# x loaded once for transposing and for the convolution, its copies to U moved to the start, and the gate's products moved back

## The chip, the cores and the metric

The kernel runs on one core of a Trainium2 chip. The core has TensorE (PE, matrix products into the PSUM accumulators), VectorE (DVE), ScalarE (ACT), GpSimd (POOL), and SyncE (SP), which here only issues transfers (DMA) between DRAM and the on-chip memory SBUF. Each engine works through its own list of instructions in order and waits on semaphores for the others. A matrix product has two operands: one is loaded as weights (PEld), the other streams through.

The metric is the device time of one execution in microseconds (us). The kernel before took 517.04 us, the median of three runs (515.87 to 517.63).

## The reference

One input x (2048 positions, 448 features) goes two ways, and a gate mixes the results:

```python
g = sigmoid((x * gate_w).sum(-1, keepdims=True))
a = attention(x)      # q = x@wq: 16 heads of 28; one k and one v head shared by all
                      # softmax(q k^T / sqrt(28)) v, then @ wo
b = ssm_conv(x)       # K[d,l] = Re sum_n C[d,n] exp(dt A[d,n])^l dt B[d,n], n < 256
                      # causal convolution of x[:,d] with K[d,:] by FFT, plus x * Dskip
return g * a + (1 - g) * b
```

Every output needs all 2048 by 2048 scores of 16 heads, that is 67 million exponentials, and for each of the 448 features a kernel K of 2048 values and a causal convolution with it.

## The kernel before, in words

**A planner.** The kernel writes its work down as operations with an engine, a cost in ns, what they read and write, and a priority (`Prog.op`, `Prog.dma`). `Prog.schedule` then plays the work through with those costs and fixes the order of instructions on each engine; what runs on the chip is that order, with semaphore waits between engines. A smaller `pr` goes first among operations that can start at the same time. `pg.after[i] = j` keeps operation i from being ordered before j without a wait on the chip. Constants such as `HEAD`, `NEED` and `AHEAD` shape the planner's choices; `PORT` charged VectorE for long GpSimd operations. So a change of a cost, a priority or a constant can reorder instructions everywhere.

**Attention.** The 2048 positions of queries are cut into 4 blocks of 512 (`qc`), the 16 heads into 4 groups of 4. For each of these 16 pairs there are 64 tiles: 16 key blocks of 128 times 4 heads. A tile's scores, 128 keys by 512 queries, fill one PSUM bank. Tiles are worked on in sets of 3 and 2 in turn (`sets`): TensorE writes their scores to banks 0 to 4, one ScalarE exponential (L1263) turns the whole set into weights `expT`, and TensorE multiplies these with the values into `psB` (L1278). The scores come in two forms: row-packed (`row`, L1231), in which heads use 32 rows each of the array and run side by side, and full-height (`full`, L1240), which reads `qM`, a copy of the queries with zeros in the other heads' rows. `qM` is filled by transfers on GpSimd's queue (L142). Sets 0 to 5 and, from set 24 on, the sets of three are row-packed. After 64 tiles `norm` divides by the sums, and `outp` and `fold` multiply with wo and the gate and add to `O`, the output in SBUF.

**The state-space part.** From the parameters VectorE builds, by repeated multiplication, tables of powers (`masters`, `tables`: L901 to L985) for 32 features at a time; TensorE makes the kernels K from them (`kgen`, L1005), which are written to DRAM (`KP_scratch`) and read back as shifted rows (`tload`, L1041); TensorE convolves with them (`conv`, L1065). The data operand is `U`, x in an order in which position residues lie side by side, with 16 zeros after each 16 values for the odd half. The results are multiplied by 1 - g (`omq`, L1080), turned (L1091) and added to `O`.

**The start.** `loads` brings x in four blocks of 512 positions, in which each partition gets 4 neighbouring rows (3584 bytes). `prep_x` transposes them on TensorE (L652), copies the results to `xT` on ScalarE and VectorE (L661, L663), makes the keys (L666, L676) with their largest absolute values (L673), and, through `Wv`, the values and the gate's sum into `psB` (L693). From the keys' maxima a bound is made (L697, L703, L704: `Wb`), which the first queries need: `qproj` makes a block's queries (L864), their absolute values (L870), the bound's product (L873) and the copy `qT` (L876). After that come the first scores and the first exponential. The copies that spread wq, wv and the gate's weights into `Wq` and `Wv` (L580 to L586) are on VectorE.

Meanwhile `prep_params` makes the seeds. The phase dt * A_im / 2 pi (L804) is brought into range by adding and subtracting a large constant (`MAGIC`) and a subtraction, both on GpSimd (L807, L808); ScalarE takes two sines (L810, L813); the cosine is 1 - 2 sin^2 of the half angle, again on GpSimd (L829, L830). The tensor dt * A_re ("t0") is another L804, `T<-psX,cst`, of which ScalarE makes six exponentials (L821, L824).

`prep_gate` makes 1 - g in the convolution's order: the value copy `vaug` (L712), the exponential (L717), three small VectorE steps (L719 to L721), then products with the identity (L736) and with selection matrices (L746) on TensorE, and the copy `omq`.

`fill` makes `U`: it loads x a second time, in the convolution's order, into `O` (16 transfers of 128 pieces of 896 bytes), and eight GpSimd copies (L611) interleave that into `U`; a transfer then copies U's even partitions to the odd ones, shifted by 16, and another clears `O`. U's zeros are four GpSimd memsets (L493, `consts`).

## Time and profile before

| | |
|---|---|
| median of three runs | 517.04 us |
| the profiled execution | 516.12 us |
| its span, first to last instruction | 514.4 us |
| ScalarE busy | 486.2 us |
| of it exponentials of scores (410 instructions) | 467.4 us |
| VectorE busy | 456.5 us |
| TensorE busy | 449.5 us |
| GpSimd busy | 176.8 us |
| first exponential of scores starts | 24.34 us |
| last exponential of scores ends | 508.2 us |
| mean granted TensorE clock | 0.959 |

How the lines are read: a timeline line gives the start and the length in us, the engine, the line of the kernel, the operation, output and input tiles with their shapes, how many instructions are merged in it, and in square brackets the engine's idle time before it and who ended that. A waits line gives the waiting instruction, what it waited for, the time in all, how often, and the longest. A line with two times and a colon is a stretch of the span with each engine's busy time in it, the granted clock, the busy share of the transfer engines, and GB/s. The granted clock is TensorE's, 1.00 being full speed.

### The profile page before, as it was taken

How to read it: one execution, taken by the hardware profiler on the slowest of the kernel's cores; microseconds unless marked ns; L12 is line 12 of the kernel's file. 1: busy time of each engine (PE TensorE's matmuls, PEld its weight loads, DVE VectorE, ACT ScalarE, POOL GpSimd, SP SyncE). 2: the span in 40 equal slices, each digit the busy share in tenths (PEclk: the TensorE clock that was granted, in tenths of full speed). 3: DMA queues.
4: the chain of work that ended last, by engine and by line, in shares of the span. 5: the costliest groups of instructions: out<-in, count | busy, mean ns of one | idle time of the engine just before them, and what ended most of it. 6: DMA issues, size and time to landing. Idle time of an engine off the chain costs nothing.

```text
span 514.4 us, 18888 instructions
## 1 busy us (share of the span) xinstructions
PE 449.5 (87%) x8456; PEld 197.2 (38%) x8456; DVE 456.5 (89%) x819; ACT 486.2 (95%) x436; POOL 176.8 (34%) x311
## 2 busy tenths in 40 slices
PE   7739779798888989989988999998899899999886
PEld 5403113143333434334443444443343444344453
DVE  4997999989999999999999999999999999821534
ACT  5677999999999999999999999999999999999995
POOL 8991122532232541424242233334252233334000
PEclk9957986979999999999999999999999999999999
DMA  9956920679989599899999999699999969999982
GB/s 238 234 146 43 135 61 22 190 215 342 354 255 303 183 335 319 269 349 290 369 337 349 348 310 368 199 313 370 369 335 331 369 204 369 286 371 330 370 284 46
DMA packets 117315, 140.29 MB, mean 273 GB/s; under 512 B 49945, under 2 KB 56506, under 8 KB 117234
## 3 DMA queue, kind: packets, MB, share of 16 engines
q1 hardware_dynamic: 108384, 129.72, 78.6%
q0 software_dynamic: 8704, 9.25, 6.8%
q8 instruction: 66, 1.08, 0.9%
q14 instruction: 15, 0.12, 0.1%
q10 hardware_dynamic: 146, 0.12, 0.1%
HBM read 127.24 MB, written 5.22 MB: 258 GB/s over the span
## 4 chain that ended last, share of the span: by engine, by line
ACT 40%; DVE 39%; PE 17%; issue 1%; DMA 1%; SPq 0%
ACT expT L1263 40%; DVE tab L958 6%; PE psS L1240 5%; PE psB L1278 3%; DVE tab L969 3%; DVE tab L970 3%; DVE msq L901 2%; PE psS L1231 2%; DVE tab L980 2%; DVE tab L968 2%; DVE tab L967 2%; DVE mbf L921 1%; DVE tmp L976 1%; DVE cst L1080 1%; DVE seedz L903 1%; DVE seedz L905 1%
## 5 line engine op out<-in xcount | busy, mean ns | idle before, releaser
L1263 ACT ACTIVATE expT<-psS 128x1536 bf16<-128x1536 f32 (+1 forms) x410 | 467.4, 1329 | 13.9 <-PE psS L1231 9.2
L1240 PE MATMUL psS<-qM,kT 128*128 128x512 bf16 (+2 forms) x481 | 134.5, 372 | 14.6 <-ACT expT L1263 13.2
L1278 PE MATMUL psB<-expT,vaug 128*32 128x512 bf16 (+2 forms) x1152 | 106.6, 375 | 3.2 <-issue 1.6
L1231 PE MATMUL psS<-qT,kT 29*128 29x512 bf16 (+2 forms) x671 | 80.6, 369 | 22.5 <-ACT expT L1263 20.0
L142 POOL DMA_DIRECT2D KP_scratch<-kstg x112 | 61.4, 556 | 60.5 <-DVE kstg L1020 42.8
L958 DVE TENSOR_TENSOR tab<-tab,mbf 128x512 bf16<-128x512 bf16 (+3 forms) x56 | 64.6, 1153 | 0.0
L1278 PEld LDWEIGHTS psB<-expT,vaug 128*32 128x32 bf16 x1152 | 27.9, 93 | 84.4 <-issue 78.6
L1240 PEld LDWEIGHTS psS<-qM,kT 128*128 128x128 bf16 x481 | 30.3, 98 | 55.4 <-ACT expT L1263 37.9
L142 POOL DMA_DIRECT2D rdenB<-R_scratch x56 | 28.6, 517 | 54.1 <-DMA R_scratch<-denT 42.8
L142 POOL DMA_DIRECT2D qM<-qT x64 | 32.7, 518 | 36.3 <-DVE qT L876 24.6
L1231 PEld LDWEIGHTS psS<-qT,kT 29*128 29x128 bf16 x671 | 20.5, 91 | 62.5 <-ACT expT L1263 48.7
L1065 PE MATMUL psX<-T,U 128*32 128x128 bf16 (+7 forms) x1760 | 42.4, 220 | 0.9 <-issue 0.8
L969 DVE TENSOR_TENSOR tab<-tab 128x128 bf16<-128x128 bf16 (+4 forms) x70 | 41.7, 596 | 0.0
L970 DVE TENSOR_TENSOR tab<-tab 128x128 bf16<-128x128 bf16 (+4 forms) x70 | 41.7, 596 | 0.0
L1065 PEld LDWEIGHTS psX<-T,U 128*32 128x32 bf16 (+7 forms) x1760 | 30.2, 93 | 21.0 <-issue 15.7
L142 POOL DMA_DIRECT2D denT<-acc x14 | 9.9, 704 | 82.3 <-DVE acc L1139 82.3
L980 DVE TENSOR_TENSOR tab<-tab,tmp 128x4096 bf16<-128x4096 bf16 x14 | 32.1, 2289 | 0.1
L968 DVE TENSOR_TENSOR tab<-tab,mbf 128x4096 bf16<-128x4096 bf16 x14 | 32.0, 2288 | 0.0
L967 DVE TENSOR_TENSOR tab<-tab,mbf 128x4096 bf16<-128x4096 bf16 x14 | 32.0, 2287 | 0.0
L142 POOL DMA_DIRECT2D R_scratch<-denT x14 | 8.2, 584 | 57.0 <-DVE denT L1131 36.2
L901 DVE TENSOR_TENSOR msq<-seedz 128x384 f32<-128x384 f32 (+1 forms) x50 | 26.9, 538 | 0.1
L976 DVE TENSOR_TENSOR tmp<-tmp,mq 128x64 bf16<-128x64 bf16 (+4 forms) x70 | 25.4, 363 | 0.1
(166 smaller groups left out, 559.0 us busy)
## 6 DMA issues: line engine op xcount, KB each, us to landing
T<-KP_scratch SPq DMA_DIRECT2D x170, 512.0 KB, 8.5
U<-KP_scratch SPq DMA_DIRECT2D x40, 512.0 KB, 9.0
tab<-KP_scratch SPq DMA_DIRECT2D x14, 512.0 KB, 9.2
rdenB<-R_scratch POOLq DMA_DIRECT2D x56, 64.0 KB, 5.5
qM<-qT POOLq DMA_DIRECT2D x64, 32.0 KB, 5.2
tab<-in_A_x_dram SPq DMA_DIRECT2D x4, 448.0 KB, 5.3
O<-in_A_x_dram SPq DMA_DIRECT2D x16, 112.0 KB, 2.8
O<-cst SPq DMA_DIRECT2D x1, 1792.0 KB, 26.4
```

Of the source, the lines that this page charges most:

```text
L142: return [e.dma_start(o, i, **kw) for o, i in pairs]
L958: vo(lambda e, dst=dst, src=src, mri=mri: e.tensor_tensor(dst, src, mri, ALU.mult), 4 * n, done + mk(lv), [kr, ki, tk])
L967: vo(lambda e, src=src, mi=mi, tv=tv: e.tensor_tensor(tv, src, mi, ALU.mult), 2 * n, done + mk(lv), [tk])
L968: vo(lambda e, dst=dst, src=src, mr=mr: e.tensor_tensor(dst, src, mr, ALU.mult), 2 * n, done + mk(lv), [kr, ki, ("gap", s)])
L969: vo(lambda e, dc=dc, tc=tc: e.tensor_tensor(dc[0], dc[0], tc[1], ALU.subtract), n, [tk, kr], [kr])
L970: vo(lambda e, dc=dc, tc=tc: e.tensor_tensor(dc[1], dc[1], tc[0], ALU.add), n, [tk, ki], [ki])
L980: vo(lambda e: e.tensor_tensor(tab.v(0, P, FM, [[4, 1024], [1, 4]]), tab.v(0, P, lo + 124, [[CG, 32], [-4, 32], [1, 4]]), rho.v(0, P, 0, [ ...
L1065: r = e.matmul(ps.v(32 * j, 32 - 2 * n, 128 * k, [[1, 128]]), self.U.v(0, P, (4 * gi + j) * 32 + 2 * n, [[1, 32 - 2 * n]]), tbuf.v(0, P, t ...
L1231: r = e.matmul(self.psS.v(0, P, 512 * b + o, [[1, n]]), kT.v(32 * h, DH + 1, 128 * kt, [[1, 128]]), qT.v(32 * h, DH + 1, 512 * (i % 2) + q ...
L1240: r = e.matmul(self.psS.v(0, P, 512 * b + o, [[1, n]]), kT.v(0, P, 128 * kt, [[1, 128]]), self.qM.v(0, P, (i % 2) * XQ + 512 * h + qo, [[1 ...
L1263: pg.op("act", lambda e: e.activation(expT.v(0, P, 512 * es[0], spread(es, n)), self.psS.v(0, P, 512 * bs[0], spread(bs, n)), AF.Exp, scal ...
L1278: r = e.matmul(self.psB.v(32 * h, 32, qo, [[1, n]]), vaug.v(0, P, 32 * kt, [[1, 32]]), expT.v(0, P, 512 * ring[t] + o, [[1, n]]), start=(k ...
```

## The change

- x is loaded once, in an order in which partitions 2r and 2r + 1 hold rows r of both halves of the positions (64 rows apart from tile to tile), in pieces of 896 bytes, each block by two transfers. The transposes' copies to `xT` put the columns back in order; the selection matrices of the gate, the turning of the convolution's results and the output transfers (two for each one before) follow the new order.
- The eight GpSimd copies to `U` read this `x` and stand ahead of most of GpSimd's memsets in the start. The second load of x is gone, and the transfer that doubles `U` and the one that clears `O` wait only for the `x` copies and the last store of `xT`.
- U's zeros become four VectorE memsets. The range step becomes two VectorE operations, and the cosine three VectorE operations (the square with -2, and two halves of the product with the added 1), in place of four GpSimd operations and one VectorE operation. The three `tiny` GpSimd operations go.
- The gate's products on TensorE are ordered behind the second `qproj`.
- The planner loses `PORT` and gains `sb`, a mark on operations which it doesn't start while a GpSimd operation runs; constants and some priorities change, and sets of three are row-packed from set 9 instead of 24.

In the resulting order TensorE's first gate product stands behind 15 sets of scores instead of 4.

```diff
-    BLOCK, FIRST, FETCH, IDLE, NEED = 256, 192, 5600.0, 3300.0, .015
+    BLOCK, FIRST, FETCH, IDLE, NEED = 256, 192, 5600.0, 3300.0, .02
-    PORT = 750.0
-    HEAD = 0.8
+    HEAD = 1.0
-    AHEAD = 3000.0
+    AHEAD = 2000.0
...
+                    if o.sb:
+                        for a, b in held:
+                            if a <= r < b:
+                                r = b
...
-                if e == "pool" and o.ns >= 900.0 and r > 25000.0:
-                    free["dve"] = max(free["dve"], r) + self.PORT
+                if e == "pool":
+                    held.append((r, free[e]))
...
-            pm(self.U.v(0, P, 16 + 3584 * k, [[32, 112], [1, 16]]), 0.0, 950, [("Uz", k)], 3.5)
+            dm(self.U.v(0, P, 16 + 3584 * k, [[32, 112], [1, 16]]), 0.0, 860, [("Uz", k)], 2.5)
...
-            pg.dma([(self.xst.v(0, P, q * 4 * D, [[1, 4 * D]]), dram(x, q * 4 * P * D, [[4 * D, P], [1, 4 * D]]))],
-                   (128, 3584), f"x{q}", wr=[("xst", q)])
+            pg.dma([(bass.AP(tensor=self.xst.h, offset=h * self.xst.rs + q * 4 * D, ap=[[2 * self.xst.rs, 64], [D, 4], [1, D]]),
+                     dram(x, (1024 * h + 256 * q) * D, [[D, 64], [64 * D, 4], [1, D]])) for h in range(2)],
+                   (512, 896), f"x{q}", wr=[("xst", q)])
...
+        for q in range(4):
+            for j in (0, 2):
+                u = 15 - 4 * q - j
+                pg.op("pool", lambda e, u=u: e.tensor_copy(
+                    self.U.v(0, P, u - 1, [[32, D], [1, 2]]),
+                    self.xst.v(0, P, (16 - u) * D, [[1, D], [-D, 2]])), 1080,
+                    rd=[("xst", q)], wr=[("uf", q, j)], pr=0.6)
...
-            lst = [(self.O.v(0, P, (8 * k + j) * D, [[1, D]]),
-                    dram(x, 64 * (15 - 8 * k - j) * D, [[D, 64], [1024 * D, 2], [1, D]])) for j in range(8)]
-            self.late.append(pg.dma(lst, (1024, 896), f"u{k}", wr=[("ust", k)], pr=0.3).i)
-            for j in range(0, 8, 2):
-                pg.op("pool", lambda e, k=k, j=j: e.tensor_copy(
-                    self.U.v(0, P, 8 * k + j, [[32, D], [1, 2]]),
-                    self.O.v(0, P, (8 * k + j) * D, [[1, D], [D, 2]])), 1080,
-                    rd=[("ust", k)], wr=[("U", k), ("ustd", k, j)] + uc, pr=1)
...
+        self.gq = [o.i for o in pg.ops[self.q1:] if o.eng == "dve"][-1]
...
+        pg.after[len(pg.ops)] = self.gq
         pg.op("pe", lambda e: e.matmul(px.v(0, 16, 0, [[1, 128]]), self.gt.v(0, P, 16, [[1, 16]]),
...
-        pg.op("pool", lambda e: e.tensor_scalar(t(2), t(1), MAGIC, -MAGIC, ALU.add, ALU.add), 900, rd=[K(1)], wr=[K(2)], pr=0.2)
-        pg.op("pool", lambda e: e.tensor_tensor(t(1), t(2), t(1), ALU.subtract), 1700,
+        pg.op("dve", lambda e: e.tensor_scalar(t(2), t(1), MAGIC, None, ALU.add), ns / 2, rd=[K(1)], wr=[K(2)], pr=0.2)
+        pg.op("dve", lambda e: e.scalar_tensor_tensor(t(1), t(2), -MAGIC, t(1), ALU.add, ALU.subtract), ns,
...
-        pg.op("pool", lambda e: e.tensor_tensor(t(4), t(4), t(4), ALU.mult), 1700, rd=[K(4)], wr=[K(4)], pr=0.3)
-        pg.op("pool", lambda e: e.tensor_scalar(t(4), t(4), -2.0, 1.0, ALU.mult, ALU.add), 900, rd=[K(4)], wr=[K(4)], pr=0.3)
-        vt(zc(0), tc(2), tc(4), ALU.mult, [K(2), K(4)], ["sz0"], 1)
+        pg.op("dve", lambda e: e.scalar_tensor_tensor(t(4), t(4), -2.0, t(4), ALU.mult, ALU.mult), ns, rd=[K(4)], wr=[K(4)], pr=0.9)
+        tz = lambda j, h: spot[j][0].v(0, P, spot[j][1] + D * h, [[32, NC], [1, 32]])
+        for h in range(2):
+            pg.op("dve", lambda e, h=h: e.scalar_tensor_tensor(self.seedz.v(0, P, 32 * h, [[64, NC], [1, 32]]), tz(4, h), 1.0, tz(2, h), ALU.add, ALU.mult),
+                  el(D), rd=[K(2), K(4)], wr=["sz0"], pr=1)
...
-        pg.dma([(dram(self.out, 15 * P * D, [[D, P], [1, D]]), self.O.v(0, P, 15 * D, [[1, D]]))],
-               (128, 896), "outl", rd=[("O", 6), ("Oz", 6)], pr=1, eng="act")
+        pg.dma(rows(15, 1, 0, D), (128, 896), "outl", rd=[("O", 6), ("Oz", 6)], pr=1, eng="act")
...
-            if s < 6 or 24 <= s < 411 and len(ts) == 3:
+            if s < 6 or 9 <= s < 411 and len(ts) == 3:
```

## The prediction

> **What bounds the kernel now.** I read, in this order, the page's busy shares, ScalarE's busy time by stage, ScalarE's timeline at the start, and the waits of the first 50 us. Of the page:
>
> ```profile
> PE 449.5 (87%) x8456; PEld 197.2 (38%) x8456; DVE 456.5 (89%) x819; ACT 486.2 (95%) x436; POOL 176.8 (34%) x311
> PEclk9957986979999999999999999999999999999999
> L1263 ACT ACTIVATE expT<-psS 128x1536 bf16<-128x1536 f32 (+1 forms) x410 | 467.4, 1329 | 13.9 <-PE psS L1231 9.2
> ```
>
> 467.4 us of the 514.4 us span are the softmax's exponentials on ScalarE. The time is therefore: start of the first exponential, plus 467.4, plus other ScalarE work after that start, plus its idle time, plus what follows the last. By stage (columns: length, then busy time of PE, PEld, DVE, ACT, POOL, granted clock, DMA):
>
> ```profile
> 24.00:45.00 21.00, 12.26 (x113) 5.12 (x109) 20.76 (x28) 14.90 (x16) 15.46 (x15) 0.52 0.53 113
> 45.00:60.00 15.00, 12.81 (x73) 3.29 (x69) 11.48 (x35) 14.99 (x13) 2.03 (x4) 0.99 0.98 69
> 60.00:115.00 55.00, 46.16 (x565) 14.55 (x569) 52.49 (x94) 53.15 (x47) 16.30 (x30) 0.81 0.46 131
> 115.00:440.00 325.00, 296.06 (x6136) 129.93 (x6129) 324.52 (x591) 323.67 (x287) 110.85 (x206) 1.00 0.95 317
> 440.00:508.20 68.20, 62.79 (x1455) 32.52 (x1454) 28.38 (x39) 65.62 (x58) 10.97 (x21) 1.00 0.89 297
> ```
>
> ScalarE idles 6.1 us between 24 and 45 us, 0.3 of them before the first exponential, and 5.8 us in all that follows. VectorE is as full from 115 to 440 us; of that below. The early idle time, in ScalarE's timeline and the waits:
>
> ```profile
> 24.34 1.45 ACT L1263 ACTIVATE expT<-psS 128x1536 bf16<-128x1536 f32 x1 [3.16 <-PE psS L1231]
> 36.73 1.45 ACT L1263 ACTIVATE expT<-psS 128x1536 bf16<-128x1536 f32 x1 [1.73 <-PE psS L1231]
> 40.52 1.02 ACT L1263 ACTIVATE expT<-psS 128x1024 bf16<-128x1024 f32 x1 [2.34 <-PE psS L746]
> ...
> PE psS L736 <- DVE gt L721: 5.4, 1, 5.4
> ```
>
> TensorE stood 5.4 us at the first gate product (L736) with the next score products queued behind it, because the gate's last VectorE step came at 34.4. It was late because VectorE was held up by GpSimd:
>
> ```profile
> 14.70 2.06 DVE L580 COPY Wq<-mbf 112x448 bf16<-112x448 bf16 x1
> 21.15 1.13 DVE L703 TENSOR_SCALAR Wb<-expT,small 128x128 bf16<-128x128 bf16 x1
> 24.76 2.15 DVE L804 TENSOR_TENSOR mbf<-T,cst 128x896 f32<-128x896 bf16 x1
> 32.14 0.99 DVE L719 TENSOR_SCALAR gt<-gt 128x16 f32<-128x16 f32 x1
> ...
> 14.55 2.08 POOL L808 TENSOR_TENSOR T<-T 128x896 f32<-128x896 f32 x1
> 17.06 6.83 POOL L493 MEMSET U<- 128x1792 bf16 x4
> 29.57 10.63 POOL L611 COPY U<-O 128x896 bf16<-128x896 bf16 x8
> ```
>
> The reader is to see that each slow VectorE row ends where a GpSimd row ends: L580 at 16.76 with L808 at 16.63; a 16-element operation (L719) takes 0.99 us beside a U copy.
>
> **Part by part.**
>
> *Start of the first exponential.* I follow VectorE from its cast at 11.50 (L663) to the end of qT's copy at 23.85; all shifts are in us.
> - x in 896-byte pieces, two transfers for one on SP: x0's second half is issued 0.46 later, x1's 0.92 (SP's spacing is 0.46). The next nearest row for such pieces is O's load: from 26 to 30 us it ran 202 GB/s at a DMA share of 0.80, so 252 GB/s when full, against 390 for 3584-byte pieces between 8 and 10 us. Four loads of 459 KB then take 7.3 instead of 4.7 us. x1 is what TensorE waits for (to 6.97); x3 is needed only at 12.3. Between 0 and +0.9 for x1: +0.4.
> - U's zeros, four memsets on VectorE ahead of the first cast: a 128-element one takes 0.14 from start to start, so 896 about 1.0 and four 3.9, from 2.1 to 6.0. VectorE was idle 2.81 until 4.88; its two casts end at about 7.3, still before ScalarE's two end at 7.8. Nothing (0 to +0.5 if the memsets are slower).
> - Range step on VectorE: the product before it and the first addition (0.5 to 1.1) fall into 1.47 of idle time before 11.50, but among U copies; +0.3 (0 to +1.4). The subtraction, 1.08 by L804's rows, stands right before the Wq copy; with a wait for a U copy of 0 to 1.13 (median copy): +1.4 (1.1 to 2.2).
> - Wq copy: 2.06 now. Free of GpSimd it lies between 0.2 (L939's 128 elements, 0.22) and 0.7 (a 512-element cast); GpSimd's L808 is gone, but late U copies or short memsets may hold it: -1.1 (-1.8 to +0.3).
> - The other weight copies and two memsets, 17.28 to 19.20, go behind the bound's two operations: -1.9. Part of them lands beside TensorE's 0.4 product before qT's copy: +0.1 (to +0.8).
> - L703 1.13 meets no long memset: -0.6 (-1.0 to 0).
>
> Together -1.4, ends -4.3 and +4.1 if all went one way; -3 to +2 is what I keep. First exponential near 22.9.
>
> GpSimd's eight U copies need 9 us (8 x 1.13) from about 6, so to 15 or, held by VectorE, 17. Its later memsets (some 5 us by the present rows) end by 23. qM's transfers (25.90 now) can then issue at 23 in 2.2; on SP, O's 16 loads of x (12.7 us) go, so U's doubling in 32-byte pieces moves from 40 to about 20 and lies beside them. The next qM transfers lay beside it and took 6.1 (median of 4, from 51.7): landed by 32, before the first full-height set near 34. Nothing.
>
> [...]
>
> *From the first exponential to 45 us.* Idle now, after the first: 0.83 + 1.73 + 2.34 + 0.33 + 0.47 = 5.7. The first gate product goes from behind 4 score sets to behind 15, the others (L746) behind 17, so the 1.73 and 2.34 go. Next late: the gate's exponential (it waits for vaug's copy, that for the 64 value products, which end 1.95 after the first exponential now): 0.4 idle. Then the product t0 (L804, 1.08) behind the gate's addition on VectorE's queue, on which now two of ScalarE's exponentials and the third set, queued behind them, wait: 1.7 idle. Then the half clock: at 0.5, a set of five tiles takes TensorE 1.39 + 0.97 + 1.25 x 0.55 = 3.0 with full-height products (rows at 40.37 to 45) against ScalarE's 2.37, 0.6 lost for each of not quite two such pairs: 1.1. 3.2 in all: -2.5 (-4.3 if the product t0 is ready, 0 if a new wait takes it all).
>
> *VectorE.* Its rows between 24.7 and 40 are stretched by about 8 us (1.1 + 0.6 + 1.0 + 0.9 + 0.7 + 0.9 + 0.8 + 0.7 + 0.6 + 0.8 over the same shapes later). GpSimd is quiet there now; the sine's square and cosine's folding add 1.1. So the tables start some 8 us earlier and don't bound.
>
> *Later.* Three-tile sets use row-packed products from the 10th set instead of the 25th. Row packing leaves TensorE emptier (0.54 against 0.76 for three at full clock), and the two clock drops after 62 us (0.57 to 0.50 at 72 to 84, 0.50 at 104) come where packing is in use, each with 0.8 of ScalarE idle. One more, partly: +0.3 (0 to +1.5). The gate products' 2 us of TensorE time (eight at 0.42) now fall into pairs with 0.87 of slack at full clock (2.37 less 0.39 + 0.61 + 0.50): 0, to +1 at half clock. The changed priorities of K's and y's products reorder TensorE throughout; 5.1 of idle time after 45 us bounds the gain, I take 0 (-1.5 to +1.5).
>
> *End.* Output in two transfers each; the last pair is on ScalarE's queue behind the last fold: one more issue at 0.39 to 0.46: +0.45. SP's pairs end before it.
>
> Sum: -1.4 - 2.5 + 0.3 + 0.45 = -3.15. The profiled execution took 516.1 (span 514.4 and 1.7 around it), so 513.0; it stands 0.9 below the median of 517.04, so I forecast 513.9 for the median.
>
> **Rivals.**
> 1. *The clock stays up.* The granted clock falls to 0.50 at 24.7 us although TensorE's longest idle before was 1.85. If in the changed kernel it doesn't, the 1.1 of half-clock loss and the slow value products (about 1) go: 511.8. For it: TensorE's new front has no 5.4 us hole. Against: the hole comes after the drop, and the waits before it stay. [...]
> 2. *The wait only moves.* The product t0 is late by as much as the gate was (raw2's transpose and VectorE's order decide), and the first exponential saves nothing after its start: 517.04 - 1.4 + 0.75 = 516.4. Against: VectorE has lost its holds there.
> [...]
> 4. *Slower: VectorE-timed products block TensorE's queue in the middle* (its order is new, and VectorE is full): idle time after 45 us doubles, 519.
>
> **How the numbers follow.** A measurement here tells 0.3%, 1.55 us, from no change. My forecast 0.50 (511.5 to 515.4), rival 1 0.18, rival 2 0.15, rival 3 0.12, rival 4 0.05. Faster than 515.5: 0.50 + 0.18 = 0.68, plus 0.01 from rival 2: 0.69. Within: 0.14. Slower than 518.6: 0.17. The range 509.5 to 518.5 takes in rivals 1 and 2 with their spread and leaves out the slower two and little below.
>
> **What would show it.** First exponential at 21.5 to 24 (wrong from 26 on); no wait of TensorE at the gate product over 1 us; Wq's copy and L703's successor under 1.2 and 0.7; ScalarE idle 2 to 4.5 between its first exponential and 45 us; VectorE's first table products near 46 to 51 instead of 58; the second output issue on ScalarE's queue 0.4 after the first. A wait of TensorE on VectorE over 2 us in the middle, or a first exponential after 26, makes the forecast wrong.

## The result and the profile after

The kernel after takes 510.89 us (median of four runs, 509.9 to 511.51), the kernel before on the same chip 516.45 us. The ratio is 0.9888, with a 95% interval from 0.9862 to 0.9915: by the medians the change saves 5.6 us, where 3.1 were forecast. The profiled execution took 510.81 us with a span of 509.0; that of before took 516.12 with a span of 514.4.

The page of the kernel after, in the lines that answer to those shown of before (share of the span, then the clock in 40 slices, then the group of the scores' exponentials):

```profile
PE 446.3 (88%) x8456; PEld 195.8 (38%) x8456; DVE 453.2 (89%) x827; ACT 484.7 (95%) x436; POOL 159.4 (31%) x302
PEclk9959788899999999999999999998999999999999
L1271 ACT ACTIVATE expT<-psS 128x1536 bf16<-128x1536 f32 (+1 forms) x410 | 466.0, 1341 | 8.4 <-PE psS L1239 4.8
```

The 410 exponentials still fill the span; GpSimd's busy time went down by 17.4 us, which by itself is worth nothing, since GpSimd isn't the limit. By stage of the kernel after (length, then busy time of PE, PEld, DVE, ACT, POOL, granted clock, DMA share, GB/s):

```profile
24.00:45.00 21.00, 13.40 (x82) 3.38 (x82) 20.25 (x44) 19.57 (x21) 0.16 (x1) 0.76 0.84 94
45.00:60.00 15.00, 11.95 (x67) 3.31 (x67) 14.96 (x42) 13.70 (x12) 1.96 (x4) 0.81 0.46 112
60.00:115.00 55.00, 45.44 (x670) 15.74 (x670) 51.28 (x101) 52.87 (x47) 19.90 (x37) 0.90 0.50 155
```

ScalarE's busy time between 24 and 45 us rose from 14.90 to 19.57 of 21 us. GpSimd, busy for 15.46 us of this stage before, now does almost nothing in it. The next stage is worse than before: 13.70 of 15 us instead of 14.99, at a clock of 0.81 instead of 0.99. ScalarE's timeline after, with its idle time in brackets:

```profile
22.16 2.37 ACT L1271 ACTIVATE expT<-psS 128x1536 bf16<-128x1536 f32 x2 [0.82 <-PE psS L1239]
24.72 0.18 ACT L721 ACTIVATE gt<-psB 128x16 f32<-128x16 f32 x1 [0.19 <-DVE vaug L716]
26.14 0.95 ACT L826 ACTIVATE T<-T 128x896 f32<-128x896 f32 x1 [1.24 <-DVE T L809]
35.66 22.13 ACT L1271 ACTIVATE expT<-psS 128x1536 bf16<-128x1536 f32 x19
58.60 1.02 ACT L1271 ACTIVATE expT<-psS 128x1024 bf16<-128x1024 f32 x1 [0.81 <-PE psS L1248]
60.66 3.71 ACT L1271 ACTIVATE expT<-psS 128x1536 bf16<-128x1536 f32 x3 [1.04 <-PE psS L1239]
```

Behind the first exponential there are two waits, 0.19 for the value copy and 1.24 for the product t0; then 32 us without one. The next come at 58 us. VectorE and GpSimd after, in the rows that were stretched before:

```profile
10.36 1.34 DVE L812 TENSOR_SCALAR T<-T 128x896 f32<-128x896 f32 x1
15.55 1.24 DVE L813 SCALAR_TENSOR_TENSOR T<-T 128x896 f32<-128x896 f32 x1
16.72 0.43 DVE L582 COPY Wq<-mbf 112x448 bf16<-112x448 bf16 x1
19.86 0.24 DVE L706 TENSOR_SCALAR Wb<-expT,small 128x128 bf16<-128x128 bf16 x1
24.93 0.17 DVE L723 TENSOR_SCALAR gt<-gt 128x16 f32<-128x16 f32 x1 [0.25 <-ACT gt L721]
27.12 0.16 DVE L725 TENSOR_SCALAR gt<-gt 128x16 f32<-128x16 f32 x1
```
```profile
5.85 10.00 POOL L606 COPY U<-tab 128x896 bf16<-128x896 bf16 x8
21.98 2.19 POOL L142 DMA_DIRECT2D qM<-qT  x4 [0.96 <-DVE qT L883]
```

The eight U copies end at 15.85, before any of the gate's steps exist. The gate's first step takes 0.17 us instead of 0.99, and its last is done at 27.3 instead of 35.4. In the kernel before, two rows of VectorE's that the readings below use are these:

```profile
29.10 3.12 DVE L804 TENSOR_TENSOR seedz<-T 128x896 f32<-128x896 f32 x2
34.42 1.00 DVE L721 TENSOR_SCALAR gt<-gt 128x16 f32<-128x16 f32 x1
```

Of the 8.1 us by which the gate is ready earlier, 2.2 are the earlier first exponential. The rest is shorter rows and also a shorter queue: between the first exponential and the gate's last step VectorE now has two of the large products, where it had four. The two kernels alone don't separate these.

The span splits into five terms: the start of the first exponential, ScalarE's busy time from there to the end of the last one, its idle time in that stretch (in three parts), and the tail from the end of the last exponential to the end of the span. Busy times and idle times come from ScalarE's busy time by stage, with the stages counted from each kernel's own first exponential.

| term (us) | before | after | difference | forecast |
|---|---|---|---|---|
| first exponential starts | 24.34 | 22.16 | -2.18 | -1.4 |
| idle, first 21 us behind it | 5.76 | 1.43 | -4.33 | -2.5 |
| idle, the next 72 us | 1.86 | 3.43 | +1.57 | +0.3 |
| idle, the rest | 3.92 | 4.09 | +0.17 | 0 |
| busy | 472.32 | 470.87 | -1.45 | 0 |
| tail | 6.19 | 6.97 | +0.78 | +0.45 |
| span | 514.4 | 509.0 | -5.4 | -3.15 |

### The profile page after: what moved, and what is told of

The parts are those of the page before. It is cut to its first block, busy times and chain, and to the rows that moved or that the text cites. A ratio compares the mean times of both kernels' runs of the same rounds, so it can differ in the third digit from the quotient of the medians.

```text
span 509.0 us, 18885 instructions
## 1 busy us (share of the span) xinstructions
PE 446.3 (88%) x8456; PEld 195.8 (38%) x8456; DVE 453.2 (89%) x827; ACT 484.7 (95%) x436; POOL 159.4 (31%) x302
## 3 DMA queue, kind: packets, MB, share of 16 engines
q8 instruction: 66, 1.08, 0.9%
## 4 chain that ended last, share of the span: by engine, by line
DVE 63%; ACT 20%; PE 13%; issue 2%; DMA 1%; SPq 1%
ACT expT L1271 19%; DVE tab L965 10%; DVE tab L976 5%; DVE tab L977 5%; DVE tab L987 5%; DVE tab L974 5%; DVE tab L975 5%; DVE tmp L983 3%; DVE msq L908 3%; PE psS L1248 3%; DVE cst L1087 2%; PE psS L1239 2%; PE psB L1286 2%; DVE seedz L912 2%; DVE mbf L928 2%; DVE seedz L910 2%
## 5 line engine op out<-in xcount | busy, mean ns | idle before, releaser
L1248 PE MATMUL psS<-qM,kT 128*128 128x512 bf16 (+2 forms) x460 | 127.8, 369 | 14.4 <-ACT expT L1271 11.9
L1239 PE MATMUL psS<-qT,kT 29*128 29x512 bf16 (+2 forms) x692 | 82.5, 367 | 30.2 <-ACT expT L1271 27.3
L1286 PE MATMUL psB<-expT,vaug 128*32 128x512 bf16 (+2 forms) x1152 | 104.8, 373 | 0.6 <-DVE acc L1146 0.4
L142 POOL DMA_DIRECT2D KP_scratch<-kstg x112 | 61.3, 555 | 39.7 <-DVE kstg L1027 25.1
L1248 PEld LDWEIGHTS psS<-qM,kT 128*128 128x128 bf16 x460 | 28.7, 98 | 52.1 <-ACT expT L1271 34.3
L1072 PE MATMUL psX<-T,U 128*32 128x128 bf16 (+7 forms) x1600 | 39.9, 220 | 3.0 <-issue 1.8
L1072 PEld LDWEIGHTS psX<-T,U 128*32 128x32 bf16 (+7 forms) x1600 | 27.4, 93 | 21.1 <-issue 13.8
L1072 PE MATMUL psS<-T,U 128*32 128x128 bf16 (+7 forms) x1120 | 28.1, 220 | 0.6 <-DVE kstg L1027 0.4
```

Of the source, the lines that this page charges most:

```text
L142: return [e.dma_start(o, i, **kw) for o, i in pairs]
L1072: r = e.matmul(ps.v(32 * j, 32 - 2 * n, 128 * k, [[1, 128]]), self.U.v(0, P, (4 * gi + j) * 32 + 2 * n, [[1, 32 - 2 * n]]), tbuf.v(0, P, t ...
L1239: r = e.matmul(self.psS.v(0, P, 512 * b + o, [[1, n]]), kT.v(32 * h, DH + 1, 128 * kt, [[1, 128]]), qT.v(32 * h, DH + 1, 512 * (i % 2) + q ...
L1248: r = e.matmul(self.psS.v(0, P, 512 * b + o, [[1, n]]), kT.v(0, P, 128 * kt, [[1, 128]]), self.qM.v(0, P, (i % 2) * XQ + 512 * h + qo, [[1 ...
L1286: r = e.matmul(self.psB.v(32 * h, 32, qo, [[1, n]]), vaug.v(0, P, 32 * kt, [[1, 32]]), expT.v(0, P, 512 * ring[t] + o, [[1, n]]), start=(k ...
```

## The experiments

Two theories could explain the gain. By the theory of holds, GpSimd instructions that ran beside VectorE's held VectorE up, so that the gate's steps came late; freeing VectorE is the gain. By the theory of order, the gain comes from standing the gate's products on TensorE behind the second block's queries, so that a late gate blocks no scores. To compare kernels I use two sums: the *start* is the first exponential plus ScalarE's idle time in the 38 us behind it (30.11 before, 25.05 after), and the *rest* is the later idle time plus the tail (11.95 before, 13.04 after). Busy time varies only between 470.9 and 472.9 in all these kernels. Each kernel was measured beside the kernel before on the same chip, and its ratio is to that. Start and rest come from one profiled execution of each kernel, and executions of one kernel differ: the 82 of the kernel before beside these runs took 511.9 to 521.2 us. A rest that differs by 2 us therefore shows little by itself; times are compared by medians and ratios.

**The gate's products in front again** (the kernel after without this part).

```diff
-        pg.after[len(pg.ops)] = self.gq
```

> The changed kernel with the gate's products put back where the planner starts them (behind 5 sets of scores). Order theory (the gain between 24 and 45 us came from taking the gate products off the head of TensorE's queue): TensorE waits 4 us or more at the first gate product again, ScalarE idles about 5.5 us between its first exponential and 45 us instead of 1.4, time about 515. Hold theory (the gate was late because GpSimd held VectorE; without holds it is ready in time): the wait at the gate product is under 1 us, ScalarE idles 2 to 3 us, time 511.5 to 512.5. Both: first exponential at 22.2.

Measured: 514.19 us, ratio 0.9974 (0.994 to 1.0008). First exponential 22.08, idle behind it 1.71 in the first 21 us, start 24.34, rest 14.95. TensorE's wait at the first gate product in this kernel (what waited for what, the sum, how often, the longest):

```profile
PE psS L740 <- DVE gt L725: 1.8, 1, 1.8
```

It is 1.8 us and not the 5.4 of before, although the product stands in front again: VectorE had made the gate early. The start is even 0.7 better than in the kernel after. So with VectorE free the early gain doesn't need the order; the theory of order falls for that stage. But the time went up by 3.3 us, and the ratio can't be told from 1: in time most of the gain is gone. The trace puts the loss in the rest (+1.9 in an execution 1.2 us below the median); its cause isn't shown.

**The U copies behind the first queries** (the kernel after, this part moved back; seven of the eight copies moved, to 22.08 us and later, and the first still ran at 12.76).

```diff
+                self.ucop = getattr(self, "ucop", []) + [len(pg.ops)]
                 pg.op("pool", lambda e, u=u: e.tensor_copy(
...
+        for i in self.ucop:
+            pg.after[i] = q0
```

> The changed kernel with the eight U copies ordered behind the first queries, so at about 23 to 34 us. Hold theory: first exponential earlier, 21 to 21.7 (range subtraction, addition and Wq copy meet fewer reading GpSimd operations), but VectorE's rows between 24 and 34 stretch by 4 to 6 us, the product t0 and with it ScalarE's exponentials are later, and idle time to 45 us rises from 1.4 to about 3; time 512. Order theory: only the first exponential moves, idle time stays at 1.4, time 510.

Measured: 515.92 us, ratio 1.0012 (0.9981 to 1.0043). Start 25.06, rest 15.90. The first exponential comes at 20.08, 2.08 earlier than in the kernel after, but ScalarE then idles 4.82 us instead of 1.43. VectorE's first rows in this kernel, and the largest of ScalarE's early waits on its timeline:

```profile
10.41 0.63 DVE L815 TENSOR_SCALAR T<-T 128x896 f32<-128x896 f32 x1
14.01 1.08 DVE L816 SCALAR_TENSOR_TENSOR T<-T 128x896 f32<-128x896 f32 x1
15.01 0.27 DVE L582 COPY Wq<-mbf 112x448 bf16<-112x448 bf16 x1
```
```profile
29.52 1.45 ACT L1274 ACTIVATE expT<-psS 128x1536 bf16<-128x1536 f32 x1 [2.71 <-DMA XS_scratch<-expT]
```

The three VectorE rows take 1.98 us without the copies beside them and 3.01 with them (1.34 + 1.24 + 0.43 in the kernel after). So the early U copies do hold VectorE ahead of the first exponential, by 1.03 us in these rows, and the first exponential is 2.08 later. That the early place repays this behind the first exponential isn't shown: of the 3.39 us by which ScalarE idles longer here, 2.71 are another thing. This kernel's new order on SP's queue issues the stores of `expT` at 21.91 us instead of 19.09, and an exponential waits 2.71 us to reuse the buffer. The two starts are the same, and the time is 5.0 us longer, of which the trace puts 2.9 in the rest without showing why.

**Range and cosine on GpSimd again** (the kernel after, this part undone).

```diff
-        pg.op("dve", lambda e: e.tensor_scalar(t(2), t(1), MAGIC, None, ALU.add), ns / 2, rd=[K(1)], wr=[K(2)], pr=0.2)
...
+        pg.op("pool", lambda e: e.tensor_scalar(t(2), t(1), MAGIC, -MAGIC, ALU.add, ALU.add), 900, rd=[K(1)], wr=[K(2)], pr=0.2)
...
+        pg.op("pool", lambda e: e.tensor_tensor(t(4), t(4), t(4), ALU.mult), 1700, rd=[K(4)], wr=[K(4)], pr=0.3)
+        pg.op("pool", lambda e: e.tensor_scalar(t(4), t(4), -2.0, 1.0, ALU.mult, ALU.add), 900, rd=[K(4)], wr=[K(4)], pr=0.3)
...
```

> The changed kernel with the range step and the cosine back on GpSimd, now behind U copies on its queue. Hold theory: the range product on GpSimd waits for U copies and ends after 17, the sines on ScalarE and with them the key copies come later, first exponential 24 to 26; the cosine's two GpSimd operations stretch VectorE by 2 to 3 us after 24; time 513 to 515. Order theory: the gate products are late in the queue all the same, idle time to 45 us stays below 2, time 511 to 512.

Measured: 515.91 us, ratio 1.0001 (0.9966 to 1.0036): the gain is gone. First exponential 23.09, start 26.22, rest 15.77. The Wq copy takes 1.40 again and the bound's two steps 0.74 and 1.15; the gate's first step takes 1.94 beside the cosine's product on GpSimd. Behind it VectorE also waits 1.27 us for the cosine itself, so this part brings back a dependency as well as holds. The start lost 1.2 and the rest 2.7.

**Row packing from set 24 again** (the kernel after).

```diff
-            if s < 6 or 9 <= s < 411 and len(ts) == 3:
+            if s < 6 or 24 <= s < 411 and len(ts) == 3:
```

> The changed kernel with sets of three row-packed from set 24 again. Clock theory (row packing from set 9 empties TensorE, the granted clock falls at 53 to 60 us and ScalarE loses 1.3 us there and about 1 at 60): no clock drop before 62 us, ScalarE's idle time from 45 to 60 us under 0.3, time 509.5 to 510. Rival (the drop comes from the start's empty TensorE, not from packing): the drop stays, no change of time within 0.5.

Measured: 511.85 us, ratio 0.9925 (0.9892 to 0.9957). Start 24.38, rest 14.57. The granted clock stayed at 1.00 from 21 to 38 us behind the first exponential, where it was 0.82 in the kernel after, and 0.62 us of idle time stood there instead of 1.46. So the earlier row packing does cost clock, some 0.8 us in that stage. The time doesn't show it: 511.85 can't be told from 510.89.

**No reading copies** (the kernel before, its order kept; x doesn't reach `U`, so the convolution's data is left out).

```diff
-                pg.op("pool", lambda e, k=k, j=j: e.tensor_copy(
-                    self.U.v(0, P, 8 * k + j, [[32, D], [1, 2]]),
-                    self.O.v(0, P, (8 * k + j) * D, [[1, D], [D, 2]])), 1080,
+                pg.op("pool", lambda e, k=k, j=j: e.memset(
+                    self.U.v(0, P, 8 * k + j, [[32, D], [1, 2]]), 0.0), 1080,
```

> The kernel before, in its own order, with the eight GpSimd copies to U replaced by GpSimd memsets of the same places: the convolution's data is left out, GpSimd is as occupied as before but reads nothing. Hold theory with the rule that reading matters: VectorE's products and its scalar-tensor-tensor operations with two SBUF inputs between 29 and 40 us fall to their unheld lengths (the seed products 1.08 instead of 1.6, L903 and L905 0.28 instead of 0.9 to 1.05), single-input ones (L719, L721, L921, L939) may stay near 1.0; the gate's last VectorE step comes at 31 to 33 instead of 35.4, TensorE's wait at the gate product falls from 5.4 to 2 to 4, ScalarE's idle time to 45 us from 5.8 to 3 to 4.5, time 1.5 to 3 below before. Rival (the slow rows are VectorE's own waits for its operands): nothing changes, same time as before.

Measured: 512.23 us, ratio 0.9929 (0.9895 to 0.9964). Start 26.39, rest 13.61. VectorE, GpSimd and TensorE's wait in this kernel:

```profile
28.82 2.28 DVE L803 TENSOR_TENSOR seedz<-T 128x896 f32<-128x896 f32 x2
31.02 0.16 DVE L718 TENSOR_SCALAR gt<-gt 128x16 f32<-128x16 f32 x1
31.13 1.03 DVE L920 CAST mbf<-seedz 128x256 bf16<-128x256 f32 x1
32.51 0.48 DVE L720 TENSOR_SCALAR gt<-gt 128x16 f32<-128x16 f32 x1
```
```profile
29.27 7.46 POOL L611 MEMSET U<- 128x896 bf16 x8
```
```profile
PE psS L735 <- DVE gt L720: 3.3, 1, 3.3
```

With the order kept and memsets in the places of GpSimd's copies, the two products take 2.28 instead of 3.12 us, the gate's last step ends at 33.0 instead of 35.4, TensorE waits 3.3 instead of 5.4, and the start is 3.7 us shorter. The ratio gives the same gain in time, 3.7 us. This is the hold without a change of order; the memsets are also shorter than the copies (7.46 us for eight instead of 10.63), so it isn't the reading alone. The hold is not all gone: beside the memsets the rows L900, L902 and L904 take at most 0.41 us, where they took up to 1.08 beside the copies (L901, L903 and L905 there), but a cast (L920) still takes 1.03 instead of 0.28. Why they differ isn't shown.

**The gate's products back, alone** (the kernel before with this part).

```diff
+        self.gq = [o.i for o in pg.ops[self.q1:] if o.eng == "dve"][-1]
...
+        pg.after[len(pg.ops)] = self.gq
```

> The kernel before with only the gate products moved behind the second query block. Hold theory: TensorE no longer waits 5.4, but VectorE is held as before; ScalarE's waits shrink by what the gate alone cost, 2 to 3 us of the 5.8, and the tables start no earlier (58 us), so part comes back as idle time later; time 513.5 to 516. Order theory: idle time to 45 us falls to about 1.5, time 511 to 512.

Measured: 520.53 us, ratio 1.0095 (1.0054 to 1.0135): slower, which neither theory had. Start 27.24, rest 20.69. Between 20 and 70 us in this kernel:

```profile
ACT expT L1265 <- PE psS L1242: 4.7, 4, 2.4
PE psS L875 <- DVE qT L872: 2.8, 1, 2.8
```

In its first 21 us behind the first exponential ScalarE idles only 0.74 us instead of 5.76, so the order alone takes the early wait away. It comes back in the next 17 us, with 4.06 us: VectorE is still held by the U copies (and waits 2.23 us for the cosine), so the second block's queries are late instead of the gate, and TensorE waits for them (L875). The start is 2.9 us better than before, the rest 8.7 worse: ScalarE waits once for 4.59 us at 366 us, where TensorE had stood 1.74 us for VectorE's folding into `O` and shorter for its other products.

**Range and cosine on VectorE, alone** (the kernel before with this part: the reverse of the diff shown above, with the three cosine operations of the change).

```diff
-        pg.op("pool", lambda e: e.tensor_tensor(t(1), t(2), t(1), ALU.subtract), 1700,
+        pg.op("dve", lambda e: e.scalar_tensor_tensor(t(1), t(2), -MAGIC, t(1), ALU.add, ALU.subtract), ns,
...
+        pg.op("dve", lambda e: e.scalar_tensor_tensor(t(4), t(4), -2.0, t(4), ALU.mult, ALU.mult), ns, rd=[K(4)], wr=[K(4)], pr=0.9)
```

> The kernel before with the range step and the cosine on VectorE as after, nothing else. Theory of holds: the Wq copy no longer stands beside a reading GpSimd product (2.06 to below 1), the product t0 and the additions near 25 us are held no more by the cosine's products; first exponential 0.5 to 1.5 earlier (putting them back in the kernel after cost 0.93); but the eight U copies still lie from 29 to 37, so the gate's steps stay held and TensorE still waits 3 to 5.5 us at the first gate product. Time 514 to 516. Rival (two more operations on a full VectorE only push the rest back): first exponential at 24 or later and a time of 516 to 518.

Measured: 511.45 us, ratio 0.9929 (0.9908 to 0.995). This part alone makes most of the gain, by the ratios about two thirds (0.71% against 1.12%), with x still loaded twice and the gate's products still in front; 514 to 516 was expected, and the U copies were to keep the gate late. First exponential 21.02, start 22.76 (the best of all), rest 13.52. On VectorE, GpSimd and TensorE's timeline of this kernel:

```profile
15.47 0.27 DVE L580 COPY Wq<-mbf 112x448 bf16<-112x448 bf16 x1
25.93 0.17 DVE L719 TENSOR_SCALAR gt<-gt 128x16 f32<-128x16 f32 x1
27.65 0.17 DVE L721 TENSOR_SCALAR gt<-gt 128x16 f32<-128x16 f32 x1
28.98 0.27 DVE L740 COPY acc<-psS 16x128 f32<-16x128 f32 x1
```
```profile
31.86 10.93 POOL L611 COPY U<-O 128x896 bf16<-128x896 bf16 x8 [8.80 <-DMA O<-in_A_x_dram]
```
```profile
27.87 0.61 PE L736 MATMUL psS<-onT,gt 128*16 128x128 f32 x2 [2.06 <-DVE gt L721]
```

The U copies come late, at 31.86, because SP issues the second load of x from 23.61 on instead of 19.07. By then the gate is through, including its copy `acc` (L740). The expectation failed at a placement: the copies weren't where the kernel before had them.

**The cosine on VectorE, alone** (the kernel before; the range step stays on GpSimd).

```diff
-        pg.op("pool", lambda e: e.tensor_tensor(t(4), t(4), t(4), ALU.mult), 1700, rd=[K(4)], wr=[K(4)], pr=0.3)
-        pg.op("pool", lambda e: e.tensor_scalar(t(4), t(4), -2.0, 1.0, ALU.mult, ALU.add), 900, rd=[K(4)], wr=[K(4)], pr=0.3)
...
+        pg.op("dve", lambda e: e.scalar_tensor_tensor(t(4), t(4), -2.0, t(4), ALU.mult, ALU.mult), ns, rd=[K(4)], wr=[K(4)], pr=0.9)
...
```

> The kernel before with the cosine alone on VectorE; the range step stays on GpSimd. Theory of holds: the Wq copy stays beside a reading GpSimd product (near 2 us) and the first exponential stays near 24 (23 to 24.8); but the two cosine products, which held the products on VectorE by about 1.7 us near 25 us, are gone, so that the gate's last step comes at 29.5 to 32 instead of 34.4; ScalarE idle 2 to 4 in the 21 us behind its first exponential (5.76 before, 1.74 with both parts on VectorE), time 513 to 515. Rival (the range step's part is what counts, by starting VectorE's work 3 us earlier, ahead of the U copies): the gate's steps meet the U copies as before, last step at 33 or later, idle 4.5 to 6, time 515.5 to 517.

Measured: 516.43 us, ratio 1.001 (0.9981 to 1.0039): no gain. First exponential 22.90, idle in the first 21 us 4.32, start 27.22, rest 14.24. VectorE, GpSimd and TensorE's timeline of this kernel:

```profile
28.19 0.17 DVE L721 TENSOR_SCALAR gt<-gt 128x16 f32<-128x16 f32 x1
28.47 1.25 DVE L902 TENSOR_TENSOR msq<-seedz 128x256 f32<-128x256 f32 x1
29.65 1.05 DVE L940 COPY tab<-mbf 128x128 bf16<-128x128 bf16 x1
32.96 0.27 DVE L740 COPY acc<-psS 16x128 f32<-16x128 f32 x1
```
```profile
28.29 9.05 POOL L611 COPY U<-O 128x896 bf16<-128x896 bf16 x8 [2.30 <-DMA O<-in_A_x_dram]
```
```profile
28.42 0.61 PE L736 MATMUL psS<-onT,gt 128*16 128x128 f32 x2 [0.73 <-DVE gt L721]
33.29 1.32 PE L746 MATMUL psS<-acc,onT 16*128 16x64 f32 x5 [4.26 <-DVE acc L740]
```

This pair of kernels shows the mechanism best. The gate's last step is as early as with both parts (28.19 against 27.65), even earlier than expected, and the first gate product hardly waits. But here the U copies start at 28.29. The next gate operation on VectorE, the copy `acc`, stands behind seven rows, four of them held, where with both parts it stood behind four and small memsets, none held; it comes at 32.96 instead of 28.98, and TensorE waits 4.26 us one product later. The wait has moved from L736 to L746. By the letter of the expectation both sides missed: the last step came early (against the rival), and the time stayed (against the theory of holds as I had put it, with the gate's last step as its mark).

**Range and cosine on VectorE, and the gate's products back** (the kernel before with these two).

```diff
+        pg.after[len(pg.ops)] = self.gq
...
-        pg.op("pool", lambda e: e.tensor_tensor(t(1), t(2), t(1), ALU.subtract), 1700,
+        pg.op("dve", lambda e: e.scalar_tensor_tensor(t(1), t(2), -MAGIC, t(1), ALU.add, ALU.subtract), ns,
...
```

> The kernel before with the seeds on VectorE and the gate's products behind the second block's queries; x is still loaded twice and the U copies still come late. Theory of holds: the U copies hold VectorE's steps of the second block's queries, so TensorE's wait only moves from the gate product to the queries, as with the gate alone (2.4 us there): ScalarE idle 4 to 6 us in the 38 us behind its first exponential, and a time of 514 to 519. Rival (seeds and gate together are the whole gain and the early x copies are not needed): idle below 3 there, and a time of 510 to 513.

Measured: 519.1 us, ratio 1.0074 (1.0052 to 1.0095). The start is 24.36, the rest 20.39. Beside the kernel with range and cosine alone (511.45), moving the gate's products back costs 7.7 us, 1.6 at the start and 6.9 in the rest (6.01 us idle behind 438 us, and a tail of 9.94). The theory of holds had the time nearly right, but not its reason: the first 38 us idle 4.3 us, as it says, and most of the loss lies at the end.

**The planner's constants back** (the kernel after; four priorities and costs of later products also go back, in lines not shown).

```diff
-    BLOCK, FIRST, FETCH, IDLE, NEED = 256, 192, 5600.0, 3300.0, .02
+    BLOCK, FIRST, FETCH, IDLE, NEED = 256, 192, 5600.0, 3300.0, .015
-    HEAD = 1.0
+    HEAD = 0.8
-    AHEAD = 2000.0
+    AHEAD = 3000.0
...
```

> The kernel after with the planner's three constants (NEED, HEAD, AHEAD) and the four priorities and costs of the later products (kernels K, their stores, y's turning, wo's products) as in the kernel before; everything done in the start is as after. Theory of the start (the gain is made before 45 us, by VectorE's freedom from GpSimd): first exponential 22 +-0.5, ScalarE's idle time in the 21 us behind it 1 to 2.5, and a time of 510 to 514, above or below 510.9 only by what the order after 60 us happens to give. Rival (the constants carry the gain by a better order later): start as after, but ScalarE idle 5 to 8 us beyond 38 us after its first exponential instead of 6.1, and a time of 514 to 517.

Measured: 513.37 us, ratio 0.9951 (0.9917 to 0.9985). First exponential 21.83, start 25.12 as in the kernel after, rest 15.45, that is 2.4 more. The start doesn't need the constants. In this one order they were worth about 2.5 us by the medians; the time fell between the two theories' best values.

**The last output on two queues** (the kernel after; then with a second edit that holds the six t0 exponentials behind the third set's).

```diff
-        pg.dma(rows(15, 1, 0, D), (128, 896), "outl", rd=[("O", 6), ("Oz", 6)], pr=1, eng="act")
+        lst = rows(15, 1, 0, D)
+        pg.dma(lst[:1], (64, 896), "outl", rd=[("O", 6), ("Oz", 6)], pr=1, eng="act")
+        pg.dma(lst[1:], (64, 896), "outm", rd=[("O", 6), ("Oz", 6)], pr=1)
```

> The changed kernel, same order, only the last two output transfers are issued on two queues, one on ScalarE's and one on SP's. If the tail's 0.8 us are the second issue on ScalarE's queue: 0.5 to 0.7 less from the last exponential's end to the end of the span (7.0 to 6.4), time 510.2 to 510.5 against 510.9. Rival (the tail is the landing): no change.

Measured: 510.63 us, ratio 0.989 (0.985 to 0.9929), a tail of 6.55 instead of 6.97. In the kernel after the pair of issues takes this, at the end of ScalarE's queue:

```profile
505.90 1.18 ACTq L142 DMA_DIRECT2D out_dram<-O  x2
```

It was 0.39 for the single one before. The tail shrank by 0.42, but the time can't be told from the 510.89 of the kernel after.

```diff
+            if s == 2:
+                for k in self.e0:
+                    pg.after[k] = len(pg.ops) - 1
...
```

> As the run before, and the exponential of t0 and the five after it are ordered behind the third set's scores. ScalarE's 1.24 us of idle time for t0's product goes, the seeds come 1.3 us later; if the early stage sets the end, another 1.0 less (509.3); if the order planned for later decides, within 1.5 of the run before in either direction.

Measured: 535.69 us, ratio 1.0375 (1.0304 to 1.0446). The idle time in the first 21 us is 1.17 and the 1.24 of the product t0 has gone, but ScalarE now waits 0.98 for the buffer that a store still reads. In TensorE's timeline of this kernel:

```profile
64.47 0.61 PE L741 MATMUL psS<-onT,gt 128*16 128x128 f32 x2 [6.44 <-DVE qT L878]
```

The planner put the gate's first product, still behind the second block's queries, in front of scores that were due; VectorE made those queries late, and TensorE stood 6.44 us with the scores behind it. Between 38 and 93 us ScalarE idles 13.43 us. No kernel here was measurably faster than the one after.

All runs together, in the order of their start (the first three columns and the profiled time are of one execution; the median and the ratio are of all):

| kernel | first exponential | start | rest | profiled, us | median, us | ratio |
|---|---|---|---|---|---|---|
| before + range, cosine on VectorE | 21.02 | 22.76 | 13.52 | 510.83 | 511.45 | 0.9929 |
| after, gate in front | 22.08 | 24.34 | 14.95 | 513.02 | 514.19 | 0.9974 |
| before + range, cosine, gate back | 20.07 | 24.36 | 20.39 | 518.88 | 519.1 | 1.0074 |
| after, row packing late | 21.52 | 24.38 | 14.57 | 513.15 | 511.85 | 0.9925 |
| after | 22.16 | 25.05 | 13.04 | 510.81 | 510.89 | 0.9888 |
| after, U copies late | 20.08 | 25.06 | 15.90 | 514.89 | 515.92 | 1.0012 |
| after, last output on two queues | 21.86 | 25.11 | 12.11 | 510.27 | 510.63 | 0.989 |
| after, constants back | 21.83 | 25.12 | 15.45 | 514.73 | 513.37 | 0.9951 |
| after + output, t0 late | 22.17 | 26.09 | 34.47 | 535.29 | 535.69 | 1.0375 |
| after, range, cosine on GpSimd | 23.09 | 26.22 | 15.77 | 516.07 | 515.91 | 1.0001 |
| before, no reading copies | 24.06 | 26.39 | 13.61 | 514.39 | 512.23 | 0.9929 |
| before + cosine on VectorE | 22.90 | 27.22 | 14.24 | 515.87 | 516.43 | 1.001 |
| before + gate back | 22.44 | 27.24 | 20.69 | 522.35 | 520.53 | 1.0095 |
| before | 24.34 | 30.11 | 11.95 | 516.12 | 517.04 | 1 |

The kernel before has the worst start and the best rest. The others pay 0.2 to 8.7 us more in the rest (one 22.5), as much as the start can bring. So the start doesn't decide the time: the eight kernels with a start of 22.8 to 25.1 us have ratios from 0.9888 to 1.0074. Some of the difference in rest is that of one execution: the kernel without reading copies keeps the order of before, and its profiled execution was the slowest of ten. What makes the rest longer where the order is new isn't shown in general; two causes were seen, in the kernel with the gate back and in the one with t0 late.

## Why the prediction was right

The direction and the stage were right, and the time lay in the range; the forecast was 3.0 us high. The cause named was right for the first exponential, and not for the larger term behind it. That the sum came so near is partly luck: errors of -0.8, -1.8 and -1.45 us in three terms stand against +1.8 in the others. By its own steps:

*First exponential* (-1.4, measured -2.18). Followed on VectorE from start to start: the last early cast is 0.37 later and the maxima behind it 0.85 later, the 0.37 included (x's smaller pieces and the range step together, 0.7 forecast); the subtraction adds 1.17 (1.4); the Wq copy saves 1.63 (1.1); the weight copies that went behind the bound save 1.93 (1.9); gaps between the steps add 0.25; the bound's first step saves 0.89 (0.6). The sum is -2.18. The terms that were mis-sized are the copies freed of holds, Wq and the bound, each taken nearer the middle of its bounds than it came out. U's zeros took 3.63 us on VectorE (3.9) and were hidden, as costed. The ends that the prediction lists for these terms add up to -3.5 and +4.2, not -4.3 and +4.1; it went on with -3 to +2, so nothing rests on that.

*From the first exponential to 45 us* (-2.5, measured -4.33). The two waits taken from the trace go, as said. Of what was to come in their place, the gate's exponential costs 0.19 (0.4) and the product t0 1.24 (1.7). The step that failed is the half clock, put at 1.1 of idle time: the clock was at half from 26.88 to 37.12 us, but that cost nothing. The prediction set the slow TensorE against score exponentials in pairs; five of t0's exponentials stood between them in these 10 us, and TensorE still waited 4.67, 0.59 and 1.57 us for ScalarE. And the reason that was given for the gain (the gate's products go behind 15 score sets, so the waits go) wasn't needed: with the products in front again the first 21 us idle 1.71 instead of 1.43. Alone it does take this wait away (0.74), but with VectorE still held 4.06 come back in the next 17 us. What keeps the wait away is the step called *VectorE* in the prediction, which was credited with nothing here: the gate was ready 8.1 us earlier. The tables begin 11.1 us earlier, at 47.17 instead of 58.30, not "some 8".

*Row packing and clock* (+0.3, ends 0 to +1.5; measured +1.57 in the 72 us behind the start). The term was mis-sized at its upper end: the clock was 0.58 from 53 to 60 us and 0.57 from 84 to 92, and ScalarE lost about 1.2 us in each. With the packing put back the 72 us idle 2.11 instead of 3.43. The prediction's 0.54 us for three row-packed products "at full clock" is a row at half clock (36.02 in the kernel before); at full clock they take 0.32 from start to the next (62.94), so packing leaves TensorE emptier still. *Later* came out at +0.17 against 0; the 5.1 us of idle time after 45 us that bounded it are 5.8 by the stages. The *end* cost +0.78 instead of +0.45, because a transfer of half the rows has an issue of 0.54 to 0.61, not 0.39 to 0.46.

The 1.45 us by which ScalarE's busy time shrank was in no term. The instructions are the same; neighbours overlap a little in the records, and there are fewer breaks between them, but that this is the reason wasn't shown.

*Rivals.* The first (the clock stays up) is wrong about the clock, which was at 0.50 from 26.88 to 37.12 us, and right in what it saves: the loss of 1.1 didn't come. The second (the wait only moves) fell for the kernel after, and is what happened with the cosine alone. The third, given 0.12 (U copies hold VectorE ahead of the first exponential), is real and small: with seven of them moved the first exponential came 2.08 us earlier, 1.03 of it in the held rows, and the other parts more than paid for it. The fourth was seen in two other kernels: TensorE stood for VectorE at 366 us in the one with the gate back and at 58 us in the one with t0 late, and their rests are 8.7 and 22.5 us longer, far above the 2 us of the rival. Its chance was taken too small for a change that replans everything.

*Readings.* The product L804 at 8.35, one of the rows of 1.08 us, stood for the most part beside an affine select on GpSimd; there GpSimd's instruction was the longer one (0.95 us instead of 0.29 for the same shape in the kernel after). And a held row doesn't always end where a GpSimd row ends: L804 at 24.76 ends at 26.91, about its own length after GpSimd's product at 25.96. The 0.3% that was to tell a change from none is too fine for single executions, which differ by more (511.9 to 521.2 us for the kernel before).

## What to carry to other kernels

Rows that last several times as long as the same shape elsewhere (the gate's first step 0.99 us against 0.17), and end where another engine's row ends or their own usual length after it, are held here, and what helped was to move the other engine's work off that stretch (later, or to another engine), not to reorder those who wait. When a wait is taken away, follow the whole chain behind it: here the gate's next copy on VectorE was enough to bring it all back. With a planner that reorders everything, a gain of 2 us in one stage must be held against what the rest does by accident: judge by stage, by many executions, and test the cause with a change that keeps the order, such as the copies replaced by memsets here.

## What the runs showed of the hardware

The granted clock fell in the kernel after soon after TensorE had run out of work at 25.49 us (columns as in the other stage lines):

```profile
26.50:27.00 0.50, 0.00 (x0) 0.00 (x0) 0.50 (x1) 0.50 (x2) 0.00 (x0) 0.88 0.96 80
27.00:28.00 1.00, 0.00 (x0) 0.00 (x0) 1.00 (x3) 1.00 (x3) 0.00 (x0) 0.50 1.03 93
53.00:60.00 7.00, 6.17 (x26) 1.22 (x26) 7.00 (x12) 5.82 (x6) 0.00 (x0) 0.58 0.08 22
84.00:92.00 8.00, 7.26 (x35) 1.52 (x33) 7.25 (x6) 6.74 (x6) 0.70 (x3) 0.57 0.85 267
```

It was at half before the hole was 1.5 us long, and from 53 to 60 and 84 to 92 us it was near half while TensorE was busy for 88 and 91% of the time. With row packing from set 24 it stayed at 1.00 from 42.5 to 59.5 us; in the kernel after it was 0.82 from 43.2 to 60.2. What makes it fall isn't shown: no run sets TensorE's busy share alone, and that row packing lowers the clock by leaving TensorE less to do is the author's reading.

Two transfers of 64 partitions each took longer to issue here than one of 128: on ScalarE's queue 1.18 us for the pair against 0.39, and on SP's 1.45 us for x's first pair against 0.40 for the one transfer before (in larger pieces).

GpSimd's rows were stretched too. In the kernel after the U copy on GpSimd at 9.12 us took 2.09 us, where the shortest took 1.03; VectorE's product beside it (L809 at 9.24) took its usual 1.08.
